# RWKV-7 attention and an exact-GELU block on one core: a new hand-written order of all steps, and a state turned with 40 weight columns

## The chip, the core and the metric

The kernel runs on one core of a Trainium2 chip. The metric is device time in microseconds. The kernel before was run three times: 655.43, 659.05 and 662.18 us, median 659.05.

## What is computed

The first half is a recurrence over 768 time steps for 4 batches and 8 heads of width 40. The second half takes its output as 3072 tokens of width 320 and puts them through two matrices with an exact GELU between.

```python
for t in range(S):                                   # S = 768, D = 40
    y[:, :, t] = einsum('bhd,bhde->bhe', rt, state)
    Sa = einsum('bhde,bhe->bhd', state, at)
    state = state * wt[:, :, None, :] - einsum('bhd,bhe->bhde', Sa, bt) \
            + einsum('bhd,bhe->bhde', vt, kt)
x = y.transpose(0, 2, 1, 3).reshape(B * S, H * D)    # (3072, 320)
h = x @ w_in                                         # w_in (320, 2048), float64
out = (0.5 * h * (1 + erf(h / sqrt(2)))) @ w_out     # w_out (2048, 320), float64
```

## The kernel before

Time is cut into 12 chunks of 64 steps, numbered 0 to 11. Within a chunk the recurrence becomes matrix products and the inverse of a triangular 64 by 64 matrix for each of the 32 pairs of batch and head. Each chunk then yields 256 tokens for the GELU block.

The kernel is written as small steps, each a Python generator whose pieces are issued one by one. `ORDER` (line 28) is a list of tokens written out by hand, such as `N9:2`: the next piece of step N of chunk 9, with duo 2 as its place. A duo is one of the four PSUM tiles of two banks (line 141); `conv` is one of three scratch tiles. The loop at line 1399 issues the tokens from left to right. Each of the engines PE, DVE, ACT, POOL and SP works its own instructions off strictly in the order in which the list brings them, and semaphores carry the dependencies between engines. The order of the list is thus the order of every queue, of SP's DMA issues too.

Steps of a chunk c that matter here, with their lines:

- `w`, `a`, `b`, `k`, `r`, `v`, `wq`, `vp`, `bp`, `kp` (246 to 311) load the inputs through SP's queue. `wi`, `wl`, `wo` load the two weight matrices (427 to 465), and `ci`, `co` turn their float64 words into float32 on DVE and ACT (492 to 502). They fill the first three chunks.
- `logs`, `sums`, `wt` (512 to 566) form the decays; `ta`, `tb`, `tk`, `tv`, `tr` (593 to 684) turn the inputs.
- `N` (714) multiplies on PE, masks on DVE (line 692), and stores the diagonal 32 by 32 blocks to DRAM with four issues. `nb` (796) loads them back with one matrix to a partition. `inv` (808) inverts them on POOL with 31 pairs of a product (line 819) and a sum (line 821) and stores the result (line 828; for chunk 3 and later POOL issues the store itself, before that SP). `ft` (837) loads the inverse, `corner` (924) turns a part on DVE (line 926) and multiplies on PE, and `joined` (938) completes the inverse `Tt`.
- `A`, `RV`, `av` (739 to 775) are products of inputs alone. `X` (955), `sa` (966), `QY`, `qk` (1047 to 1054) use the state; `state` (1107) writes the next one.
- `tn` (991) turns the state with PE and copies it to `turned` on ACT; `yy` (1020) multiplies with it, and `y` (1057) writes the tokens and moves some of their rows by DMA, partly through DRAM.
- `ph` (1205) is x @ w_in, from chunk 3 on with 7 half products for 8 (`pc`, `pd`, `pg` copy, add and apply the GELU); `po` (1286) is the product with w_out, from chunk 2 on likewise with sums on DVE.
- `warm` and `begin` (1382 to 1393) are products without use that keep PE going.

Every float32 product shows as two MATMUL records, a transpose as one. A group of 32 small products is thus 64 records.

Of the kernel before, what the change touches and what calls it, by code (L numbers as in the profile page):

```python
# [36 lines left out]
r2 tn1:2 r2 wi1 wi1 sc2 A1:0 A1 co0 y0:3 ci4:1 tables0 sums2 y0:1 y0 y0 RV1:0 wi1 wi1 RV1 ci4 inv1 tn1 tr2:1
tr2 ta2:2 co0 co1 tb2:0 ta2 av1:1:3 tb2 zeros8 yy1:2 inv3 wo2 yy1 ci4 ci6:0 yy1 ci6 k2 ci7:1 inv1 co1 inv2 wi1 v2
ci6 ci8:2 ph0:0 X1 N2:2 sk2 X1 ph0 ft1 N2 ci8 corner1:0 X1 ph0 ph0:1 corner1:2 ci8 ph0 ci7 wo4 ft1 zeros6 tk2:0 zeros7
corner1 co3:0 co3 co5:2 co5 co3 wo9 zeros5 ft1 ci7 tv2:2 co2:0 N2 tables0 co9:1 kp3 wo6 N2 a3 wq3 a3 wo15 tails1 kp3  # L40
tk2 A2:3 w3 nb2 wq3 nb2 b3 wo8 w3 A2 tv2 inv2 inv2 RV2:0 tables1 inv2 k3 inv2 RV2 co2 co2 co7:0 co9 ph0
ph0:2 joined1:0 joined1 ph0 co5 co7 co7 ph0 ph0:1 joined1 co4:0 sa1:0:2 co4 ta3 co6:2 ph0 sa1 sa1 co6 QY1:0:3 qk1 co6 co4 y1
state1 po0:2 co8:0 ph0 po0 co8 tn2:3 wo10 tn2 wt3:2 av2:0:1 co8 yy2:3 co9 y1 y1 wt3 co11:0 co11 yy2 yy2 wt3 logs3 y1
po0 po0 bp3 wt3 co15:1 vp3 co11 bp3 y1 vp3 vp3 tb3 wo14 tk3:2 co15 ta3 vp3 X2 ph1:3 co10:2 ph1 co14:0 X2 ph1
ph1:0 ph1 a4 N3:3 co10 tv3 a4 co14 wo12 co14 X2 wo13 co15 ph1 N3 co12:1 wq4 wq4 co12 co10 co12 sums3:1 ph1:0 r3
N3 ph1 N3 co13:2 inv2 r3 nb3 nb3 sums3 sk3 A3:3 inv4 co13 co13 wt4:1 ft2 ta4 inv3 po1:1 sc3 wt4 r3 ft2 ft2
po0 po0 corner2:2 ph1 po0 po0 A3 corner2:0 corner2 po1 joined2:0 vp4 ph1:3 wt4 r3 po0 po0 joined2 joined2 v3 tr3 sa2:0:2 bp4 ph1
w4 ph1 sa2 sa2 QY2:0:2 qk2 y2 state2 po1 bp4 RV3:3 RV3 po1 inv3 w4 vp4 vp4 po0 vp4 tv4 wt4 y2 kp4 kp4
tn3:2 av3:3:0 tn3 yy3:2 tb4 yy3 y2 y2 po1 yy3 X3 a5 ta4 tk4:1 wq5 po0 N4:2 inv3 po1 N4 y2 po1 wq5 N4
wt5:1 ph2:2 X3 ws0 N4 inv3 inv3 ph2 wt5 ph2 ph2:3 ph2 ph2 r4 r4 ph2:2 ww0:2 ww0 nb4 nb4 inv4 wt5 ft3 logs4  # L50
ft3 inv4 ft3 corner3:0 ph2 ws1 ww0 ph2 corner3:3 corner3 po1 ws3 joined3:3 r4 a5 r4 po1 ph2:2 po1 vp5 vp5 ws2 joined3 joined3
vp5 A4:1 ta5 X3 tr4 po1 sa3:3:0 sa3 sa3 ph2 vp5 A4 bp5 RV4:3 v4 kp5 ph2 kp5 QY3:0:1 qk3 inv4 po2:0 sums4:2 RV4
po2:3 y3 state3 sums4 k4 po2 tv5 b4 bp5 wt5 po2:1 tn4:1 po2 po2 y3 y3 av4:0:2 inv4 tn4 yy4:1 y3 ta5 yy4 yy4
tb5 wq6 po2:3 po2 N5:1 po1 wq6 a6 po2 po2 po2 X4 a6 N5 inv4 po2:3 y3 wt6:1 tk5:0 N5 N5 po2 X4 X4
po2 po2 po2:2 ft4 po2 nb5 tx3 tx3 sk4 tx3 A5:3 wt6 wt6 sc4 ph3:2 ft4 corner4:0 ft4 ph3:0 corner4:1 ta6 pc3 nb5 r5
pd3 tx3 ph3 inv5 corner4 tx3 joined4:0 pc3 r5 inv6 w5 A5 joined4 joined4 vp6 ph3:1 sa4:0:3 ww0 vp6 pg3 r5 bp6 ph3 pc3
sa4 r5 sa4 pd3 QY4:3:0 qk4 state4 tr5 ph3 pg3 w5 ph3 pd3 v6 pg3 y4 RV5:1 tn5:3 pg3 po3:0 po3:2 po3 vp6 inv5
RV5 logs5 v5 vp6 sums5:1 tn5 wt6 tv6 po3:1 po3 sums5 po2 yy5:3 yy5 ta6 inv5 kp6 yy5 av5:2:0 inv5 bp6 tb6 po3 po3:1
po3 po3 po3 po3 b5 inv5 kp6 po3:3 po3 y4 y4 N6:1 y4 tx4 a7 po3 wq7 wq7 tx4 N6 y4 tx4 a7 po3
inv5 X5 X5 N6 N6 k5 ft5 nb6 nb6 ph4:3 X5 ft5 ft5 sc5 pc4 ph4:0 ph4 pc4 wt7:1 wt7 ph4:2 ph4 sk5 tk6:0  # L60
r6 tx4 pd4 r6 inv6 corner5:0 ta7 corner5:0 r6 po3:1 inv6 inv6 wt7 po3 pg4 w6 corner5 po3 w6 warm4:0 tx4 pc4 joined5:1 joined5
# [14 lines left out]
ta10 ph7:1 r9 ph7 ft8 r9 pc7 ph7:0 ph7 ft8 r9 pc7 corner8:2 pd7 corner8 tx7 pd7 warm7:1 sk8 sc8 v9 vp10 joined8:2 joined8  # L76
r9 joined8 bp10 bp10 ph7 inv9 inv9 tx7 pd7 pg7 vp10 sa8:2:1 sa8 po6 ph7 w9 vp10 sa8 QY8:1:2 qk8 tr9 pg7 pg7 pg7
kp10 RV9:3 vp10 y8 state8 RV9 po7:0 po7:0 po7 tn9:2 y8 tv10 av9:3:1 wt10 po7:1 tn9 po7 po7 inv9 w9 ta10 y8 y8 yy9:0
yy9 wq11 po7:2 po7 yy9 po7 logs9 tx8 inv9 po7 po7 tx8 tx8 wq11 wt11:1 b9 tb10 po7:0 po7 kp10 sums9:2 wt11 po7 sums9
X9 tk10:0 inv9 N10:0 inv9 N10 X9 X9 k9 y8 ft9 sk9 ft9 ph8:2 N10 ph8:1 pc8 wt11 N10 ph8 corner9:0 corner9:0 ft9 pd8  # L80
r10 tx8 po7 corner9 po7:1 po7 joined9:0 nb10 nb10 sc9 inv10 joined9 joined9 r10 r10 tx8 pc8 ph8:3 sa9:0:1 sa9 inv11 r10 inv10 pg8
sa9 ph8 a11 a11 QY9:1:0 qk9 pc8 pd8 ph8 ta11 tr10 pd8 ph8 y9 w10 state9 pg8 pg8 po8:0 po8:3 pg8 po8 A10:0 k10
A10 wt11 tn10:1 RV10:2 vp11 po7 RV10 tn10 po8:1 po8 po8 po8:0 w10 yy10:2 kp11 bp11 v10 bp11 yy10 kp11 yy10 av10:3:1 po8 po8
vp11 inv10 po8 tb11 y9 y9 y9 logs10 tx9 po8 po8:2 vp11 vp11 ta11 tx9 inv10 po8 N11:0 X10 X10 po8 sums10:2 N11 y9
b10 X10 N11 ph9:0 N11 inv10 ph9:1 po8 pc9 nb11 tk11:1 r11 nb11 tx9 sums10 ph9 pc9 ph9:2 ph9 pd9 tv11 sc10 ft10 ft10
corner10:1 ft10 po8:1 pc9 sk10 w11 w11 corner10:3 po8 A11:1 corner10 r11 joined10:3 joined10 pd9 tx9 tx9 pg9 ph9 joined10 pd9 r11 pg9 pg9
po9:1 ph9 v11 sa10:2:3 sa10 r11 sa10 pg9 po8 tr11 po9:0 QY10:3:2 qk10 k11 logs11 A11 inv11 y10 po9 po9:0 inv11 po9 po9 po9:1
# [1349 lines left out]
```

## Time and profile before

| | |
|---|---|
| three runs, median | 659.05 us (655.43 to 662.18) |
| profiled execution, span | 653.2 us (its time outside the span is not given) |
| PE busy | 633.2 us |
| POOL busy | 387.0 us |
| DVE busy | 483.1 us |
| ACT busy | 274.7 us |
| granted TensorE clock, mean | 0.997 |
| DMA issues on SP's queue | 721 |
| ACT table loads in the program | 51 |
| products on PE in the program | 7112 |

The profile is one execution. In a timeline row stand the start in us, the duration in us, the engine, the line, the operation, the tiles written and read, the shape and the number of records; in brackets the idle time before it and what ended that. A line 154 is a helper's, so PE's steps are told apart by their tiles: `aT,nT` is N, `st,aT` is X, `ident,st` is tn, `conv,N` and `conv,spare` are corner, `Tt,Js` is joined. A row of the waits has the total in us, the number of times and the longest. In a row of the chain that ended last stand the start, the duration and what was at work.

### The profile page before, as it was taken

How to read it: one execution, taken by the hardware profiler on the slowest of the kernel's cores; microseconds unless marked ns; L12 is line 12 of the kernel's file. 1: busy time of each engine (PE TensorE's matmuls, PEld its weight loads, DVE VectorE, ACT ScalarE, POOL GpSimd, SP SyncE). 2: the span in 40 equal slices, each digit the busy share in tenths (PEclk: the TensorE clock that was granted, in tenths of full speed). 3: DMA queues.
4: the chain of work that ended last, by engine and by line, in shares of the span. 5: the costliest groups of instructions: out<-in, count | busy, mean ns of one | idle time of the engine just before them, and what ended most of it. 6: DMA issues, size and time to landing. Idle time of an engine off the chain costs nothing.

```text
span 653.2 us, 31493 instructions
## 1 busy us (share of the span) xinstructions
PE 633.2 (97%) x14128; PEld 573.0 (88%) x14128; DVE 483.1 (74%) x643; ACT 274.7 (42%) x327; POOL 387.0 (59%) x797
## 2 busy tenths in 40 slices
PE   9998999989999999999999999999999999999997
PEld 5887788766888989999989989999999998998987
DVE  1697999997687997875976988886895874834442
ACT  4365574553334333515534345444433445135130
POOL 5258624865857865846857856868834877811000
PEclk9999999999999999999999999999999999999999
DMA  9999989568576776877776767696577865330100
GB/s 128 167 173 182 192 182 177 134 148 148 106 141 118 137 129 123 150 141 114 141 145 116 134 115 146 126 162 129 111 132 146 134 125 96 60 71 5 31 12 21
DMA packets 299111, 80.76 MB, mean 124 GB/s; under 512 B 287688, under 2 KB 292560, under 8 KB 298976
## 3 DMA queue, kind: packets, MB, share of 16 engines
q1 hardware_dynamic: 297872, 76.23, 63.5%
q0 software_dynamic: 864, 2.36, 2.1%
q8 instruction: 110, 1.80, 1.2%
q14 instruction: 25, 0.20, 0.1%
q10 hardware_dynamic: 240, 0.16, 0.1%
HBM read 65.40 MB, written 11.01 MB: 117 GB/s over the span
## 4 chain that ended last, share of the span: by engine, by line
PE 65%; POOL 10%; DMA 8%; SPq 6%; DVE 5%; issue 4%; ACT 2%; DVEq 0%; POOLq 0%; ACTq 0%
PE duo L154 25%; PE duo L1310 15%; PE duo L1216 10%; PE duo L1191 6%; SPq L222 6%; POOL tmp L819 5%; POOL W L821 5%; PE duo L1294 4%; PE duo L1223 3%; PE duo L572 2%; DMA Tt<-inv 2%; DMA inv<-W 2%; DMA Nb<-N 1%; DMA rows<-in_k_dram 1%; DMA inv<-rT 1%
## 5 line engine op out<-in xcount | busy, mean ns | idle before, releaser
L819 POOL TENSOR_TENSOR tmp<-W,Nb 128x56 f32<-128x56 f32 (+22 forms) x155 | 77.5, 500 | 60.5 <-DMA Nb<-N 48.7
L1310 PE MATMUL duo<-w_out_sb,gt 128*128 128x160 f32 x640 | 93.2, 302 | 1.9 <-ACT gt L1268 1.2
L819 POOL TENSOR_TENSOR tmp<-rT,Nb 128x56 f32<-128x56 f32 (+22 forms) x155 | 71.3, 460 | 35.7 <-DMA Nb<-N 23.9
L1310 PEld LDWEIGHTS duo<-w_out_sb,gt 128*128 128x128 f32 x640 | 87.7, 190 | 5.0 <-ACT gt L1268 1.4
L821 POOL TENSOR_TENSOR W<-W,tmp 128x56 f32<-128x56 f32 (+22 forms) x155 | 77.2, 498 | 12.1
L821 POOL TENSOR_TENSOR rT<-rT,tmp 128x56 f32<-128x56 f32 (+22 forms) x155 | 74.1, 478 | 12.1
L1216 PE MATMUL duo<-xt,w_in_sb 64*128 64x128 f32 x864 | 61.5, 275 | 0.0
L1254 ACT COPY gt<-duo 128x1024 f32<-128x1024 f32 x27 | 27.3, 1011 | 72.9 <-PE duo L1216 46.3
L1260 DVE TENSOR_TENSOR gt<-gt,duo 128x1024 f32<-128x1024 f32 x27 | 32.8, 1213 | 32.9 <-ACT gt L1254 17.3
L1223 PE MATMUL duo<-xt,w_in_sb 64*128 64x128 f32 x576 | 56.2, 272 | 0.0
L1191 PE MATMUL duo<-xt,w_in_sb 64*128 64x256 f32 x480 | 55.6, 382 | 0.6 <-ACT SM L962 0.4
L1216 PEld LDWEIGHTS duo<-xt,w_in_sb 64*128 64x128 f32 x864 | 54.1, 188 | 1.7 <-DVE spare L692 0.5
L1191 PEld LDWEIGHTS duo<-xt,w_in_sb 64*128 64x128 f32 x480 | 45.3, 187 | 7.6 <-ACT SM L962 0.8
L1310 PE MATMUL duo<-extra,conv 128*128 128x160 f32 x320 | 46.8, 302 | 0.5 <-issue 0.5
L1310 PEld LDWEIGHTS duo<-extra,conv 128*128 128x128 f32 x320 | 43.9, 190 | 1.6 <-issue 0.9
L1223 PEld LDWEIGHTS duo<-xt,w_in_sb 64*128 64x128 f32 x576 | 44.1, 188 | 0.0
L621 POOL TENSOR_TENSOR rows<-rows,w_tile 128x640 f32<-128x640 f32 x9 | 15.6, 1737 | 43.6 <-ACT w_tile L537 29.4
L1266 ACT ACTIVATE gt<-gt 128x1024 f32<-128x1024 f32 x27 | 28.2, 1056 | 29.3 <-DVE gt L1260 29.0
L1294 PE MATMUL duo<-w_out_sb,gt 128*128 128x320 f32 x128 | 37.0, 440 | 0.5 <-ACT w_tile L537 0.5
L1294 PEld LDWEIGHTS duo<-w_out_sb,gt 128*128 128x128 f32 x128 | 23.5, 190 | 10.2 <-ACT w_tile L537 0.6
L1314 DVE TENSOR_TENSOR os<-os,duo 128x160 f32<-128x160 f32 x40 | 12.7, 317 | 24.9 <-PE duo L1310 22.2
L962 ACT COPY SM<-duo 128x832 f32<-128x832 f32 (+1 forms) x22 | 17.4, 827 | 26.8 <-PE duo L154 26.8
(257 smaller groups left out, 1420.1 us busy)
## 6 DMA issues: line engine op xcount, KB each, us to landing
Nb<-N SPq DMA_DIRECT2D x18, 256.0 KB
VR<-in_v_dram SPq DMA_DIRECT2D x24, 160.0 KB
out_dram<-os SPq DMA_DIRECT2D x45, 80.0 KB
rows<-in_b_dram SPq DMA_DIRECT2D x22, 160.0 KB
rows<-in_k_dram SPq DMA_DIRECT2D x22, 160.0 KB
w_out_sb<-in_moe_w_out_dram SPq DMA_DIRECT2D x5, 640.0 KB
w_tile<-in_w_dram SPq DMA_DIRECT2D x36, 80.0 KB
Tt<-inv SPq DMA_DIRECT2D x44, 64.0 KB
```

Of the source, the lines that this page charges most:

```text
L154: nc.tensor.matmul(o, lhsT, rhs, start=first, stop=True, skip_group_check=True)
L222: queue[0].dma_start(out=out, in_=in_)
L819: eng.tensor_tensor(t, W[:, :nr, j:j + 1].to_broadcast([P, nr, rest]), Nb[:, j:j + 1, j + 1:].to_broadcast([P, nr, rest]), ALU.mult)
L821: eng.tensor_tensor(W[:, :nr, j + 1:], W[:, :nr, j + 1:], t, ALU.add)
L1191: nc.tensor.matmul(pt[:, x, s], w_in_sb[half(x), kt, p * P:(p + 1) * P], xt[half(x), kt], start=kt == 0, stop=kt == NK - 1)
L1216: nc.tensor.matmul(out_of(pt)[:, x, j], left(kt, j)[half(x)], right[half(x), kt], start=first and j == 0 and kt == 0, stop=True, skip_grou ...
L1223: nc.tensor.matmul(out_of(pt)[:, x, j], w_in_sb[half(x), NP, at:at + P], xt[half(x), NP, cols], start=False, stop=True, skip_group_check=True)
L1254: nc.scalar.copy(block_of(f, g), out_of(of(c)["u"]))
L1260: nc.vector.tensor_tensor(block_of(f, g), block_of(f, g), out_of(of(c)[v_]), ALU.add)
L1266: nc.scalar.activation(block_of(f, g), block_of(f, g), ACT.Gelu)
L1294: nc.tensor.matmul(pt[:, g], gt[:, f, g * P:(g + 1) * P], w_out_sb[:, f], start=f == 0, stop=f == NF - 1)
L1310: nc.tensor.matmul(pt[:, n, :DM // 2], l_[:, f], r_[:, f], start=f == 0, stop=f == NF // 2 - 1)
```

## The change

Two edits.

First, `tn` for chunks 3 and later. Its 32 products turn 40 by 40 pieces of the state: the state's columns are the weights, an identity of 40 columns streams through. Before, 64 weight columns were loaded for each piece, so that 64 rows came out, of which later steps read 40. Now 40 columns are loaded, and the copy covers partitions 0 to 103.

```diff
-                        mm(pt[half(g), x, e * NP + i], st[half(x, D), e, i, g, :HP], ident[half(x, D), half(x, D)])
+                        mm(pt[half(g, D), x, e * NP + i], st[half(x, D), e, i, g, :D], ident[half(x, D), half(x, D)])
...
-        nc.scalar.copy(turned[:, :TW].rearrange("p (n x d) -> p x n d", x=2, d=D), pt)
+        nc.scalar.copy(turned[:HP + D, :TW].rearrange("p (n x d) -> p x n d", x=2, d=D), pt[:HP + D])
```

Second, `ORDER` is replaced as a whole. The same 1554 tokens stand in it, in another order and with other places. All instructions are the same but tn's; the program has 53 ACT table loads in place of 51 and 108 separate semaphore waits on PE in place of 96. A few lines around the inversion of chunk 9, before and after:

```diff
-y7 RV8:0 inv8 inv8 bp9 y7 tn8:3 pg6 po5 po6 wt9 tn8 RV8 tv9 po6:0 av8:3:0 tb9 y7 y7 po6 inv8 yy8:2 kp9 ta9
-kp9 yy8 wq10 po6 po6:1 wq10 po6 yy8 N9:2 po6 po6 po6 X8 X8 N9 po6:1 tk9:0 y7 N9 N9 po6 logs8 wt10:1 inv8
-b8 tx7 tx7 po6 po6 po6:3 sums8:1 po6 inv10 wt10 nb9 tx7 nb9 wt10 X8 A9:0 A9 ft8 a10 corner8:0 a10 sums8 ph7:3 pc7
...
+po6 y7 yy8 tb9 k8 logs8 po6:0 y7 kp9 yy8 po6 inv8 po6 po6 X8 N9:3 po6 inv8 X8 N9 sums8:0 inv8
+po6:2 wt10:0 inv8 wt10 sums8 y7 tk9:1 po6 N9 tx7 N9 ph7:3 tx7 pc7 po6 sc8 r9 ft8 sk8 nb9 tx7 ph7:0
+corner8:1 ph7 nb9 pd7 pc7 a10 inv9 po6 ft8 ph7:2 wt10 ph7 w9 tx7 X8 vp10 ft8 po6:0 r9 po6 pc7 corner8:1
```

What the new order moves, as far as the prediction speaks of it:

- In PE's queue, between N(c) and the product of corner(c). Chunk 2: out go a piece of ph0, the first quarter of po1 and four quarters of po0; in come X1 and a warm product. Chunk 4: out go two quarters of po1 and a half product of po2; in comes X3. Chunk 5: out go X4 and three pieces of ph4; in comes a half product of po3. Chunk 7: out goes X6. Chunk 9: out go X8 and two pieces of ph8 (one of 48 records, one of 32). Chunk 10: in come two half products of po7 and one small step.
- In SP's queue: from the first store of N2 to the first load of nb2 there are 10 issues (18 before); the store of inverse 2 stands ahead of N3's stores (behind before); the first pair of ft8 stands ahead of nb9 (behind before), and the first pair of ft3 between the two loads of nb4 (behind both before). The first issues are wi1, w0, w1, a0, b1, b0 (before: w0, w1, b0, a0, r0, b1). v11 moves from po8's and po9's steps to the last steps.

More of the change, by code (lines that the diff above doesn't have):

```diff
@@ L37 @@
[L37 to L61, printed above, removed]
@@ L77 @@
[L77 to L86, printed above, removed]
@@ new lines @@
+yy3 av3:3:2 yy3 tb4 tables1 po1 y2 po1 ta4 N4:1 inv3 wq5 X3 w4 po1 wq5 N4 wt5:0 w4 X3 po1 tk4:1
+a5 y2 X3 inv3 N4 N4 ph2:1 ws3 inv3 inv3 wt5 vp5 ph2 nb4 ph2 ww0:2 ft3 nb4 corner3:1 ph2:3 a5 ph2
+inv4 corner3:2 r4 ta5 corner3 ph2 ft3 po1 ft3 vp5 ph2:1 ph2 joined3:2 wt5 ph2 bp5 inv4 A4:0 joined3 r4 ph2:3 joined3
+r4 sa3:1:2 r4 A4 v4 ph2 tr4 kp5 RV4:0 po1 sa3 sa3 vp5 RV4 po1 inv4 QY3:1:2 logs4 ph2 qk3 sums4:0 po2:1
+state3 vp5 po2:3 sums4 tn4:0 po2 b4 y3 av4:1:2 bp5 kp5 wt5 tv5 ta5 po2:0 tn4 po2 yy4:0 y3 y3 po2 yy4
@@ new lines @@
+A9 w9 logs9 QY8:1:0 kp10 RV9:2 RV9 vp10 inv9 qk8 pg7 state8 bp10 y8 warm7:3 po7:1 b9 po7:2 inv9 av9:3:1 tn9:0 kp10
+bp10 wt10 inv9 y8 po7 tn9 yy9:0 ta10 v10 po7:0 po7 yy9 y8 vp10 po7 po7:2 yy9 po7 po6 y8 tb10 inv9
+X9 k9 po7 N10:0 po7 X9 po7 sums9:2 tv10 tk10:1 tx8 y8 po7:3 sums9 sk9 N10 X9 ft9 tx8 wq11 ft9 corner9:0
+po7 ph8:2 ft9 tx8 po7 corner9:1 pc8 wq11 corner9 N10 ph8:0 a11 ph8 pc8 pd8 tx8 wt11:1 tx8 joined9:3 po7 joined9 a11
+po7:1 wt11 sc9 ph8:0 joined9 po7 inv10 N10 sa9:3:1 ph8 r10 sa9 sa9 nb10 QY9:3:1 nb10 wt11 pc8 qk9 r10 r10 pd8
@@ new lines @@
+ph8 state9 pd8 ph8 po7 r10 pg8 tr10 pg8 y9 pg8 A10:0 po8:0 ta11 po8:3 tn10:1 pg8 RV10:2 po8 wt11 tn10 inv11
+RV10 po8:1 inv10 po8 kp11 po8 vp11 inv10 po8:1 w10 yy10:2 A10 ta11 yy10 po8 vp11 y9 inv10 po8 po8 po8 av10:3:0
+y9 bp11 po8:1 vp11 bp11 y9 vp11 kp11 tx9 k10 po8 tb11 y9 yy10 tk11:0 w10 po8 inv10 N11:2 X10 X10 X10
+tx9 N11 b10 logs10 ph9:1 tx9 pc9 ph9:3 tx9 pd9 sums10:2 po8 N11 po8:0 N11 ph9 inv10 r11 nb11 ph9:3 pc9 sums10
+ph9 pc9 ft10 tv11 nb11 ft10 r11 corner10:1 corner10:2 corner10 po8 pd9 r11 tx9 pg9 ft10 A11:0 ph9 joined10:2 sc10 A11 sk10
@@ L94 @@
+po10:0 po10 po10 y11 po10 po10 po10:3 tx11 po10 ph11:2 y11 y11 tx11 po10 ph11:1 po10 tx11 y11 pc11 tx11 pd11 ph11
+tx11 ph11:0 pc11 pg11 ph11 po10:3 pc11 v11 po11:1 pd11 pg11 po10 ph11 ph11 pd11 pg11 pg11 po11:1 po11 po10 po11:0 po11
+po11 po11:3 po11 po11 po11 po11 po11:0 po11 po11 po11 po11 po11:2 po11 po11
 """
```

77 lines of the change are left out of this document (50 added, 27 removed).

## The prediction

> **What bounds the kernel now.** I read the page's busy times first, then who waited for whom, then the chain that ended last and the timelines of PE, POOL, SP and DVE around the steps that have moved.
>
> ```profile
> span 653.2 us, 31493 instructions
> PE 633.2 (97%) x14128; PEld 573.0 (88%) x14128; DVE 483.1 (74%) x643; ACT 274.7 (42%) x327; POOL 387.0 (59%) x797
> ```
>
> PE is busy for 97% of the span, and the two programs hold the same 7112 matrix products. A new order can therefore win only what PE now loses in waits, while it can lose any amount. What it loses now, 15 rows in all:
>
> ```profile
> PE duo L154 <- issue: 5.4, 6, 3.0
> ...
> PE duo L154 <- DVE w_in_sb L1388: 1.5, 1, 1.5
> ...
> PE duo L154 <- DMA Tt<-inv: 0.2, 1, 0.2
> ```
>
> The 15 rows add up to 15.8 us. 1.5 of them are the first memset, which no order avoids; 14.3 us are left to win.
>
> The one long dependency that PE's filler work must cover in every chunk is the inversion: N(c) on PE, its mask on DVE, four stores to DRAM and two loads on SP's queue, 62 small operations on POOL, a store, the loads of ft(c), a turn on DVE, and then corner(c) on PE. Chunk 10 shows it; the first row is N10 from PE's timeline, the others are from the chain that ended last, where the one but last is the inverse's way to DRAM and the last begins with corner10:
>
> ```profile
> 480.82 1.16 PE L154 MATMUL duo<-aT,nT 40*64 40x64 f32 x64 [0.17 <-DVE os L1314]
> ```
> ```profile
> 533.83 5.38 DMA inv<-W
> ...
> 544.44 2.53 PE duo L154 x164
> ```
>
> That is 63.6 us from N10 to corner10. Other engines wait for the same chain in most chunks (total, times, longest):
>
> ```profile
> POOL tmp L819 <- DMA Nb<-N: 72.6, 9, 19.5
> DVE conv L926 <- DMA Tt<-inv: 18.8, 8, 5.8
> ```
>
> POOL stood waiting for its matrix nine times and DVE for the inverse eight times, so in most chunks the chain runs without slack and PE only just has enough other work.
>
> **Part 1: PE's order between N(c) and corner(c).** The times of four windows now, N first and corner second (chunks 2, 4, 7, 9):
>
> ```profile
> 83.56 1.11 PE L154 MATMUL duo<-aT,nT 40*64 40x64 f32 x64
> ...
> 157.26 0.75 PE L154 MATMUL duo<-conv,N 32*32 32x32 f32 x64
> ```
> ```profile
> 183.37 1.11 PE L154 MATMUL duo<-aT,nT 40*64 40x64 f32 x64
> ...
> 246.74 0.75 PE L154 MATMUL duo<-conv,N 32*32 32x32 f32 x64
> ```
> ```profile
> 328.37 1.16 PE L154 MATMUL duo<-aT,nT 40*64 40x64 f32 x64
> ...
> 390.92 0.75 PE L154 MATMUL duo<-conv,spare 32*32 32x32 f32 x64 [0.34 <-DVE conv L926]
> ```
> ```profile
> 425.71 1.16 PE L154 MATMUL duo<-aT,nT 40*64 40x64 f32 x64
> ...
> 488.37 0.75 PE L154 MATMUL duo<-conv,spare 32*32 32x32 f32 x64
> ```
>
> They last 73.7, 63.4, 62.5 and 62.7 us. Chunk 7's corner already makes PE wait 0.34 us for DVE: 62.5 is a tight chain. Now the prices of the steps that the new order takes out of these windows or puts in:
>
> ```profile
> 202.75 2.42 PE L1294 MATMUL duo<-w_out_sb,gt 128*128 128x320 f32 x8
> 205.10 0.75 PE L154 MATMUL duo<-Tt,Js 32*32 32x32 f32 x64
> ...
> 210.66 2.43 PE L1191 MATMUL duo<-xt,w_in_sb 64*128 64x256 f32 x20
> ```
> ```profile
> 484.47 0.61 PE L1216 MATMUL duo<-xt,w_in_sb 64*128 64x128 f32 x8
> ...
> 485.14 0.61 PE L1216 MATMUL duo<-xt,w_in_sb 64*128 64x128 f32 x8
> ...
> 486.48 1.95 PE L1216 MATMUL duo<-rT,rows 64*128 64x128 f32 x32
> ...
> 489.05 2.44 PE L1310 MATMUL duo<-extra,gt 128*128 128x160 f32 x16
> ```
> ```profile
> 285.51 1.61 PE L154 MATMUL duo<-st,aT 40*64 40x104 f32 x64
> ```
>
> In that order: a quarter of an early po costs 2.35 us from start to start (those of po0 and po1 lie a little lower), a piece of an early ph 2.2 to 2.4, ph's 48-record piece 2.68 (four times 484.47 to 485.14), its 32-record piece 1.8 to 1.9, a half-product of a later po 2.4, and X, whose last record runs a little into the next group, 1.5.
>
> Chunk 2 loses ph0's second piece, the first quarter of po1 and four quarters of po0 (13.3 us) and gains X1 and a warm-up product (2.5): 73.7 becomes 62.9. Chunk 4 loses two quarters of po1 and one half-product of po2 (6.7) and gains X3 (1.5): 63.4 becomes 58.2. Chunk 7 loses X6: 62.5 becomes 61.0. Chunk 9 loses X8 and two pieces of ph8 (6.0): 62.7 becomes 56.7. Chunk 5 loses 5.5 by the same count, but chunk 4's stall at its corner falls inside that window and covers it. The other windows lose 2.2 us at most or grow, and I cost them at nothing.
>
> How long is the chain in the new order? POOL's operations stay as they are. Chunk 2 has waits on SP's queue that the new order takes out (N's first store and the first load back; POOL's last operation and the store of its result):
>
> ```profile
> 88.38 0.83 SPq L222 DMA_DIRECT2D N<-N  x2
> ...
> 101.61 2.33 SPq L222 DMA_DIRECT2D Nb<-N  x2
> ```
> ```profile
> 142.28 0.23 POOL L821 TENSOR_TENSOR W<-W,tmp 128x16 f32<-128x16 f32 x1
> ```
> ```profile
> 146.52 1.29 SPq L828 DMA_DIRECT2D inv<-W  x2
> ```
>
> The 18 issues from 88.38 to 101.61 become 10, about 5 us less; and the store, which stood 4 us behind N3's stores, comes ahead of them. So 73.7 becomes about 64.7, and PE waits 64.7 - 62.9 = 1.8. For the others I keep the chain that was measured: chunk 4 waits 63.4 - 58.2 = 5.2, chunk 7 1.5, chunk 9 6.0. Sum 14.5.
>
> Two bounds. The shortest chain in the trace is that of chunk 11, late, when few transfers run:
>
> ```profile
> 526.84 1.16 PE L154 MATMUL duo<-aT,nT 40*64 40x64 f32 x64
> ```
> ```profile
> 584.19 0.71 DVE L926 STREAM_TRANSPOSE conv<-Tt 128x512 f32<-128x512 f32 x1
> ```
>
> It could have started corner11 at 584.9, after 58.1 us. With 58.1 everywhere, chunk 9 alone waits, 1.4 us. Upwards, SP's order makes chunk 9 worse:
>
> ```profile
> 435.98 1.58 SPq L222 DMA_DIRECT2D Nb<-N  x2
> 438.84 0.84 SPq L222 DMA_DIRECT2D Tt<-inv  x2
> ```
>
> The load of Nb for chunk 9 was issued 2.9 us before ft8, which waits for inverse 8. In the new order ft8's first pair stands ahead of it, so POOL would begin inverse 9 up to 4 us later. In chunk 4 one of the two Nb loads likewise stands behind ft3.
>
> **Part 2: waits that go.** Where PE comes later than before, some of the 14.3 us are over by then. I take a third, 4.5 us; the ends are 0 and 14.3.
>
> **Part 3: 40 weight columns.** tn(c) for c of 3 to 11, nine times 32 products. The rows, each group running to the start of the next:
>
> ```profile
> 265.12 1.16 PE L154 MATMUL duo<-rT,late 40*64 40x64 f32 x64
> 266.10 1.09 PE L154 MATMUL duo<-ident,st 40*64 40x40 f32 x64
> 267.12 4.61 PE L1310 MATMUL duo<-w_out_sb,gt 128*128 128x160 f32 x32
> ...
> 297.97 0.75 PE L154 MATMUL duo<-conv,spare 32*32 32x32 f32 x64
> 298.65 1.62 PE L1310 MATMUL duo<-extra,gt 128*128 128x160 f32 x10
> ```
>
> tn streams only 40 columns, yet takes 1.02 us, no less than the group before it that streams 64 (0.98): with 64 weight columns, the loads set its pace. 64 records with 32 weight columns take 0.68. On the line between, 40 columns cost 0.76: 0.26 saved, nine times 2.3 us. Ends: 0 (the pace is something else) and 9 x 0.34 = 3.1. The Trainium skill, page "TensorE: Matmul & The Clock Gate", speaks against the gain in its section "Wait — 56ns, not 53.3ns?": start to start never falls below about 25 ns however few columns stream. By that rule 64 records would need 1.6 us, the saving would be 0 and the sum 2.3 us higher; the trace disagrees, since 0.68 us for 64 records is 10.6 ns each. The copy of the turned state goes to 104 partitions in place of 128 with as many elements in each, so I cost it at nothing.
>
> **Part 4: the start, and ACT.**
>
> ```profile
> 5.56 1.28 ACT L514 ACT_TABLE_LOAD   x1 [5.56 <-DMA w_tile<-in_w_dram]
> ```
>
> ACT's first operation waits for w0, now SP's first transfer. In the new order a piece of w_in goes ahead of it, and b0 is the fifth pair of loads in place of the third. One issue is about 0.75 us (435.98 above: 1.58 for two), and the piece's bytes share the way; against that, PE's warm-up covers some of it. I take +0.7, one issue (ends 0 and twice that). ACT gets two more table loads, 1.28 us each; at 42% busy it hides them (ends 0 and 2.6). PE waits on a semaphore by itself 12 times more (108 for 96); the 5.4 us that PE stood without a reason shown, over 96, bound that at 0.06 us each, 0.7, and I take 0. The load of v11, which chunk 11 does not need, moves on SP from among po8's and po9's steps to the last ones: 1.6 us for two issues that the last products cover. The remaining moves on DVE and ACT have no row that prices them; I cost them at nothing, with DVE's slack (74% busy) as cover; if that is gone, PE's waits for DVE, now among the 14.3 us, grow.
>
> **Sum.** 14.5 - 4.5 - 2.3 + 0.7 = +8.4 us on the span of 653.2. The three runs before have a median of 659.05, 5.9 above that span, so I add the difference to the median: 667.5 us.
>
> **Rivals.**
> Longer chain: ft8 ahead of Nb9 costs its 4 us, and chunk 2's front gains only half of its 9 us, so 4.5 more. 667.5 + 8.5 = 676. For it: SP issues back to back around N9. Against it: inverse 8 may end earlier relative to N9 than now.
> No change: chains of 60.5 us, midway between 58.1 and the tight 62.5 to 63.6. Chunk 4 waits 2.3, chunk 9 3.8, the others nothing: 6.1 - 4.5 - 2.3 + 0.7 = 0, 659.
> Faster (the other side): the chain reaches chunk 11's 58.1 us in all chunks because SP serves N, Nb and ft sooner. It decides once the chain is under 60.5. 1.4 - 4.5 - 2.3 + 0.7 = -4.7, 654; with twice as much of the old waits gone, 650. Against it: nowhere but in chunk 11, with the transfers nearly over, is it that short.
>
> **How the numbers follow.** Forecast (667.5, itself 662 to 672) 0.36, longer chain 0.18, no change 0.28, faster 0.18. About 1%, 6.6 us, is what a measurement here can tell from none: 652.5 and 665.6. Slower by more: 0.30 of the forecast's 0.36, and the longer chain's 0.18, 0.48 together. Faster by more: somewhat under the faster rival's share, 0.14. Within: 0.38. The range runs from 652, where the chain is short, to 677, where SP's order lengthens it; one end each keeps a tenth outside.
>
> **What would show it.** Right: in the new trace PE's or PEld's waits for DVE L926 or Tt<-inv come to 8 to 15 us, with single waits of some us ahead of corner4 and corner9, and tn's groups last near 0.76 us. Wrong: corner4 and corner9 come 58 us after N4 and N9 with no wait (then the chain has slack that I denied it), or the new waits lie in the first 150 us, or tn still lasts 1.02.

## The result, and the profile after

| | before | after |
|---|---|---|
| four runs each, median | 660.62 us (655.43 to 666.76) | 682.50 us (676.81 to 685.14) |
| profiled execution: time, span | -, 653.2 us | 685.14, 683.4 us |
| PE busy | 633.2 us | 645.5 us |
| granted TensorE clock, mean | 0.997 | 0.983 |

The ratio is 1.036, 95% interval 1.032 to 1.041: slower, by 21 to 27 us where 8.4 were forecast. The runs of a kernel vary by 1%: the profiled execution of after is the slowest of its four and that of before a quick one, so the traces are 30.2 us apart where the medians are 21.9 apart, and the trace of the second kernel in experiment 5, a disturbed execution, is not used.

First the page of after, its first lines:

```profile
span 683.4 us, 31517 instructions
...
PE 645.5 (94%) x14128; PEld 579.5 (85%) x14128; DVE 480.9 (70%) x643; ACT 276.7 (40%) x329; POOL 384.9 (56%) x797
```

The span grew by 30.2 us. 12.3 of that are PE's busy time, though PE does the same products and tn got shorter; the other 17.9 are PE's waits. The waits of after, longest first (18 rows in all, their sum 33.7 us; before 15 rows and 15.8):

```profile
PE duo L160 <- DVE conv L932: 8.5, 4, 4.2
PE duo L160 <- issue: 7.9, 4, 5.2
PE duo L160 <- DMA Tt<-inv: 3.4, 4, 1.3
PE duo L578 <- DVE extra L619: 2.2, 1, 2.2
PE duo L1316 <- ACT os L1341: 2.1, 1, 2.1
```

The first and the third row, 11.9 us, are the end of the inversion's chain (the turn ahead of corner, the inverse ahead of joined). The second is PE standing with nothing shown that it waits for. Where they lie, from PE's timeline:

```profile
70.22 3.04 PE L160 MATMUL duo<-VR,extra 64*64 64x104 f32 x60 [5.23 <-issue]
...
211.34 0.87 PE L160 MATMUL duo<-conv,spare 32*32 32x32 f32 x49 [4.16 <-DVE conv L932]
...
257.85 0.75 PE L160 MATMUL duo<-conv,N 32*32 32x32 f32 x64 [1.12 <-DVE conv L932]
264.02 1.24 PE L160 MATMUL duo<-Tt,Js 32*32 32x32 f32 x64 [1.07 <-DMA Tt<-inv]
...
316.04 0.90 PE L160 MATMUL duo<-Tt,Js 32*32 32x32 f32 x60 [1.33 <-DMA Tt<-inv]
...
509.89 0.75 PE L160 MATMUL duo<-conv,spare 32*32 32x32 f32 x64
...
572.17 0.74 PE L160 MATMUL duo<-conv,N 32*32 32x32 f32 x64 [2.76 <-DVE conv L932]
```

These are qk0, corner3, corner4, joined4, joined5, corner9 and corner10. The long waits stand at corner3 and corner10, whose windows the prediction had costed at nothing; corner4 waits 1.1 us and corner9 not at all. At corner10 the chain itself is longer: from N10 (501.78) to the issue of its Nb load (519.86) it takes 18.1 us, where before took 11.0 (480.82 to 491.78). The mask on DVE came 5.5 us after N10 (2.5 in before), and the four stores, in a row in before, are split: the second pair stands at 515.34, behind three pairs of other transfers.

And the part of the loss that no list of waits shows. The windows view of after for the five stretches in which the granted clock (the third number from the right) was halved; behind the length of the stretch stands PE's busy time:

```profile
18.20:21.60 3.40, 3.40 (x67) 1.83 (x65) 0.60 (x1) 0.99 (x1) 0.00 (x0) 0.50 1.15 152
55.70:59.10 3.40, 3.40 (x38) 3.07 (x34) 1.64 (x3) 2.78 (x4) 2.93 (x7) 0.50 1.22 132
69.40:76.20 6.80, 5.98 (x99) 4.23 (x101) 3.25 (x8) 0.70 (x2) 5.55 (x17) 0.50 0.52 87
209.30:216.10 6.80, 4.76 (x82) 4.03 (x84) 2.59 (x4) 1.30 (x2) 2.64 (x10) 0.50 1.07 143
574.50:577.90 3.40, 3.40 (x38) 3.40 (x36) 0.97 (x1) 1.19 (x2) 2.71 (x9) 0.50 0.18 31
```

PE was busy for 20.9 us in them, at half speed: 10.5 us lost by that count. The records that begin in them took 20.6 us, and at their mean durations in before they would take 10.0. Before had one such stretch, 1.7 us, behind its longest wait:

```profile
62.29 0.48 PE L154 MATMUL duo<-VR,extra 64*64 64x104 f32 x9 [3.04 <-issue]
```
```profile
63.30:66.70 3.40, 3.40 (x35) 2.02 (x29) 3.40 (x9) 0.23 (x1) 2.85 (x8) 0.50 1.24 168
```

The longer ones of after stand at the long waits: 69.4 inside that of 5.23, 209.3 inside that of 4.16, 574.5 behind that of 2.76. So the 30.2 us are: waits +17.9, halved clock +8.8, tn -1.9, and +5.4 of other PE busy time that I could not assign.

### The profile page after: what moved, and what is told of

It is laid out like the page before. It is cut to its first block, busy times and chain, and to the rows that moved or that the text cites. A ratio compares the mean times of both kernels' runs of the same rounds, so it can differ in the third digit from the quotient of the medians.

```text
span 683.4 us, 31517 instructions
## 1 busy us (share of the span) xinstructions
PE 645.5 (94%) x14128; PEld 579.5 (85%) x14128; DVE 480.9 (70%) x643; ACT 276.7 (40%) x329; POOL 384.9 (56%) x797
## 4 chain that ended last, share of the span: by engine, by line
PE 45%; POOL 20%; DMA 11%; SPq 11%; issue 7%; DVE 5%; ACT 1%; DVEq 0%; POOLq 0%; ACTq 0%
PE duo L160 19%; SPq L228 11%; PE duo L1316 10%; POOL tmp L825 10%; PE duo L1222 7%; POOL rT L827 5%; POOL W L827 5%; PE duo L1197 5%; DMA Nb<-N 4%; PE duo L1229 2%; PE duo L1300 1%; PE duo L578 1%; DMA Tt<-inv 1%; DMA inv<-W 1%; DMA inv<-rT 1%
## 5 line engine op out<-in xcount | busy, mean ns | idle before, releaser
L825 POOL TENSOR_TENSOR tmp<-W,Nb 128x56 f32<-128x56 f32 (+22 forms) x155 | 71.3, 460 | 70.0 <-DMA Nb<-N 58.3
L825 POOL TENSOR_TENSOR tmp<-rT,Nb 128x56 f32<-128x56 f32 (+22 forms) x155 | 76.2, 491 | 47.6 <-DMA Nb<-N 35.8
L827 POOL TENSOR_TENSOR W<-W,tmp 128x56 f32<-128x56 f32 (+22 forms) x155 | 81.4, 525 | 12.1
L827 POOL TENSOR_TENSOR rT<-rT,tmp 128x56 f32<-128x56 f32 (+22 forms) x155 | 72.7, 469 | 12.1
L1222 PE MATMUL duo<-xt,w_in_sb 64*128 64x128 f32 x864 | 62.5, 276 | 0.0
L1229 PE MATMUL duo<-xt,w_in_sb 64*128 64x128 f32 x576 | 58.0, 276 | 1.2 <-DVE xt L1188 1.2
L1197 PE MATMUL duo<-xt,w_in_sb 64*128 64x256 f32 x480 | 57.1, 391 | 0.0
L1222 PEld LDWEIGHTS duo<-xt,w_in_sb 64*128 64x128 f32 x864 | 54.7, 188 | 2.2 <-issue 1.3
L1197 PEld LDWEIGHTS duo<-xt,w_in_sb 64*128 64x128 f32 x480 | 47.5, 192 | 6.8 <-ACT gt L1201 0.5
L1229 PEld LDWEIGHTS duo<-xt,w_in_sb 64*128 64x128 f32 x576 | 45.4, 190 | 1.7 <-DVE xt L1188 1.6
```

The lines of the kernel that those rows point to most:

```text
L825: eng.tensor_tensor(t, W[:, :nr, j:j + 1].to_broadcast([P, nr, rest]), Nb[:, j:j + 1, j + 1:].to_broadcast([P, nr, rest]), ALU.mult)
L827: eng.tensor_tensor(W[:, :nr, j + 1:], W[:, :nr, j + 1:], t, ALU.add)
L1197: nc.tensor.matmul(pt[:, x, s], w_in_sb[half(x), kt, p * P:(p + 1) * P], xt[half(x), kt], start=kt == 0, stop=kt == NK - 1)
L1222: nc.tensor.matmul(out_of(pt)[:, x, j], left(kt, j)[half(x)], right[half(x), kt], start=first and j == 0 and kt == 0, stop=True, skip_grou ...
L1229: nc.tensor.matmul(out_of(pt)[:, x, j], w_in_sb[half(x), NP, at:at + P], xt[half(x), NP, cols], start=False, stop=True, skip_group_check=True)
```

## The experiments

All ratios are to before on the same chip, with 95% intervals; 1% is 6.6 us. "Lag" is how far PE is behind its own work at a place: the start of a step there less the sum of all earlier steps' durations, each at its mean duration, waits left out, in before's trace (tn's shorter groups in that of experiment 1).

**1. The edit of tn alone**, run twice.

```diff
-  mm(pt[half(g), x, e * NP + i], st[half(x, D), e, i, g, :HP], ident[half(x, D), half(x, D)])
+  mm(pt[half(g, D), x, e * NP + i], st[half(x, D), e, i, g, :D], ident[half(x, D), half(x, D)])
```

> The order before, with the edit of tn alone (40 weight columns from chunk 3 on). Record's part 3 (nine groups shorter by 0.26 us each): 2.0 to 2.3 us faster than before, tn groups of 0.7 to 0.8 us in place of 0.91 to 1.02. Rival (a product does not get shorter with fewer weight columns): no change.

> The order before with the edit of tn alone again, as the base for the three kernels beside it on the same chip. First run: 0.9978 of before, interval 0.9938 to 1.0019. Part 3 on record: 2.0 to 2.3 us faster, 0.9965. If it is no change: 1.000.

Measured 0.9978 (0.9938 to 1.0019) and 1.0008 (0.9979 to 1.0037): no change that can be told. The groups did get shorter, as here in the second run, where tn runs to the start of the next group:

```profile
264.70 0.81 PE L154 MATMUL duo<-ident,st 40*40 40x40 f32 x64
265.45 1.76 PE L1310 MATMUL duo<-w_out_sb,gt 128*128 128x160 f32 x11
```

0.75 us where it was 1.02. The nine groups sum to 6.1 us in the first run, 8.7 in before. In both traces PE's wait inside X6 was 2.0 to 2.2 us (0.89 before) and was followed by a halved stretch, 1.7 us, that before does not have:

```profile
330.84 0.67 PE L154 MATMUL duo<-st,aT 40*64 40x104 f32 x20 [1.96 <-issue]
```

So in these traces 2.6 us were saved and about as much was given back at one place. The saving is 0.4% of the time, and the intervals are too wide to show or to exclude it.

**2. The head and the rest, apart.** The first product of N2 is the cut. First the order of before up to the cut, then what is left in the order of after (the diff is to before, at the cut):

```diff
-ci8:2 ph0:0 X1 N2:2 sk2 X1 ph0 ft1 N2
+ci8:2 ph0:2 X1 tails1 ci7 zeros6 ph0 ph0 ci7 N2:1 sk2 co3:1 N2
...
```

> The order before up to the first product of N2, then all that is left in the order after. In the trace of after, PE stands 11.6 us further behind its own work at N2 than in the trace of before, and about 19 us more are lost after it. If the start's loss adds up (start theory): 11 to 12 us faster than after, about 671. If the later loss is waits for the chain of a chunk that would only begin earlier by as much, or that swallow the start's loss (corner theory, as on record: the loss lies at the corners and nowhere else): within 3 us of after, 680 to 684.

The other way round (the diff is to after):

```diff
-ph0 ph0 ci7 ci8:2 N2:1 co1:0 inv1 sk2 co3:1 N2
+ph0 ph0 ci7 ci8:2 warm0:1 co1:0 co1 inv3 inv1 co1 inv2 X1 N2:0 sk2 X1 ft1 N2
...
```

> The order after up to the first product of N2, then all that is left in the order before; tn as after. Start theory, loss adds up: before plus 11.6 minus 2.2, about 670. If the waits behind it swallow the start's loss: about 658 to 661.

Measured 1.0404 (1.0319 to 1.049) and 1.0166 (1.0091 to 1.024). Read together these looked as if the rest costs everything and the head 12 us more. But both kernels have a flaw: I gave the steps PSUM places by the rest's list, so that the head had the places of the other order. In the first of them PE's lag grew by 6 us more between N1 and qk0 than in before. Experiment 3 measures that.

**3. Places alone.** The order before with tn's 40 columns; ahead of N2 the steps take the PSUM places that after gives them.

```diff
-gaps0 sums0:0 sums0:1 v0
+gaps0 sums0:1 sums0:2 v0
...
-sc0 sums1 ta0 tb0:0 warm1:3 r0 warm6:1 sc1
+sc0 sums1 ta0 tb0:1 warm1:2 r0 warm6:2 sc1
```

> The order before with tn's 40 columns, in which alone the PSUM places of 40 odd tokens ahead of N2 are those that after gives to the same steps. The first run with before's head had these places and lost 6 us more between N1 and QY0 than before, with 3.5 us of PE's waits for ACT's copy of w_in_sb. If the places cost what that run showed: 4 to 7 us slower than with 40 columns alone, about 1.006 of before. Rival (the waits behind it swallow it): no change.

Measured 1.0169 (1.012 to 1.0218): some 10 us from place numbers alone. In its trace (of an execution of 660.5 us) PE's lag at N2 is 14.9 us, 8.0 with the own places. In its first 90 us PE waits 7.2 us for ACT and DVE, against nothing but the first memset's 1.5 with the own places: a place that another order would have free is still being read here. Places belong to an order; this says nothing against those of after in their own order, but it spoils the second experiment.

**4. The head with its own places.** Once more after's head and before's rest, and that with the first loads in the sequence of before.

```diff
-ci6 ph0:0 k2 tables0
+ci6 ph0:2 k2 tables0
...
-co1 inv2 X1 N2:0 sk2 X1 ft1 N2
+co1 inv2 X1 N2:2 sk2 X1 ft1 N2
```

> The order and the PSUM places of after up to the first product of N2, then all that is left in the order and the places of before; tn with 40 columns. The earlier kernel with this head had other places in it, and alien places alone cost 1.7% in another kernel. In the traces of after, PE was 11 us further behind its work at N2 than in before, 6 to 7 at N4. Start theory: 6 to 11 us slower than before with 40 columns alone (1.000), 1.009 to 1.017. Rival (nearly all of that is swallowed or was due to places): under 1.005.

```diff
-consts0 wi1 w0 logs0 w1 a0 b1 b0 sums0:1 wi0 sums0:2
+consts0 w0 w1 logs0 b0 a0 r0 b1 sums0:1 a1 sums0:2
```

> The kernel beside it (head of after with its own places, rest of before), in which the first loads stand in SP's queue in the sequence of before (w0, w1, b0, a0, r0, b1, a1, wi1, wi0). If the late b0 sets the head's loss: sc0 starts 2.5 to 3 us earlier and the kernel is 3 to 5 us faster than the one beside it. Rival: within 2 us of it.

Measured 1.0099 (1.0064 to 1.0134) and 1.0145 (1.0091 to 1.0199). The head costs 6 us, at the low end, and the late b0 is not what makes it so: with the loads as before sc0 begins at 14.27 (16.34 without that) and nothing is won. The same edit had been tried on the flawed kernel:

> The kernel with the head of after and the rest of before (1.017 of before), in which the first loads stand in SP's queue in the sequence of before: w0, w1, b0, a0, r0, b1, a1, wi1. Start theory: sc0 starts at 13.3 us in place of 16.1, N1 3 us earlier, and 3 to 5 us faster than that kernel, about 1.011 of before. Rival (the head's loss lies in PE's order and places between N1 and N2): within 2 us of that kernel.

Measured 1.0205 (1.0148 to 1.0262), no gain either. What the head of after does show, in this kernel as in after, is the longest wait "for nothing" at the same instruction, the fifth record of qk0:

```profile
68.49 2.80 PE L154 MATMUL duo<-VR,extra 64*64 64x104 f32 x60 [4.40 <-issue]
```

**5. SP's sequence.** First for all chunks, then from chunk 4 on alone. Only issues of nb, ft, N's stores (and inverse 2's) move, among themselves. For chunks 4 and 11, the second kernel:

```diff
-ph2 nb4 ph2 ww0:2 ft3 nb4 corner3:1
+ph2 nb4 ph2 ww0:2 nb4 ft3 corner3:1
...
-r11 nb11 ph9:3 pc9 sums10 ph9 pc9 ft10 tv11 nb11 ft10
+r11 nb11 ph9:3 pc9 sums10 ph9 pc9 nb11 tv11 ft10 ft10
```

> The order after, in which only the issues of nb, ft, the stores of N and the store of inverse 2 stand in SP's queue in the sequence of before among themselves; the other engines' queues are those of after. SP theory (in chunks 4, 6, 9, 10, 11 loads of the inverse stand ahead of nb or of N's stores and make the chain from N to corner longer): from N's end to the inversion's start 13 to 16 us in place of 18 to 22, and 6 to 10 us faster than after, about 674. Corner theory (steps of PE are gone from the windows, the chain's length is as before): within 2 us of after.

> The order after, in which the issues of nb, ft and N's stores stand in SP's queue in the sequence of before among themselves, from nb4 and ft3 on alone (the run before this one had that for all chunks: from N4 on it lost 12 us less than after, and between N2 and N4 it lost 12 us more). SP theory: 11 to 13 us faster than after, about 1.018 of before, with 58 us from N4 to corner4 in place of 64.4 and 62 to 63 from N11 to corner11 in place of 66.2. Corner theory: as after, 1.036 of before.

Measured 1.0356 (1.0281 to 1.043) and 1.0244 (1.0211 to 1.0277). The first looks like nothing and is two effects that cancel: its lag grows by 10 us between N2 and N4, where after's is flat (20.0 and 18.7), and from N4 to corner11 by 17 where after's grows by 29. Most of the 10 us is a wait of 8.2 us at corner2, and the clock was halved for 10.2 us from 152.6 on. In chunks 2 and 3 the new sequence is the better one; from chunk 4 on it costs. The second kernel keeps the better half and is 1.2% faster than after. Chunk 4 shows the mechanism. SP in after, then POOL's first operation on the loaded matrix:

```profile
202.63 0.45 SPq L228 DMA_DIRECT2D Nb<-N  x1
207.88 0.84 SPq L228 DMA_DIRECT2D Tt<-inv  x2
208.77 0.49 SPq L228 DMA_DIRECT2D Nb<-N  x1
```
```profile
212.75 0.23 POOL L825 TENSOR_TENSOR tmp<-W,Nb 128x31 f32<-128x31 f32 x1 [6.88 <-DMA Nb<-N]
```

and the same two in the kernel that has before's sequence in all chunks:

```profile
206.44 1.09 SPq L222 DMA_DIRECT2D Nb<-N  x2
207.62 1.07 SPq L222 DMA_DIRECT2D Tt<-inv  x2
```
```profile
211.30 0.23 POOL L819 TENSOR_TENSOR tmp<-W,Nb 128x31 f32<-128x31 f32 x1 [18.68 <-DMA Nb<-N]
```

In after the second half of Nb stands behind ft3, which waits some 5 us for inverse 3, and POOL for it. From N4 (193.41 and 198.88) to POOL's first product it takes 19.3 us in after, 12.4 here. N4 to corner4 falls from 64.4 to 57.7 in this kernel. (In the two kernels built on the mended one, experiments 7 and 11, it is still 62: there ft4 stands on SP behind the stores of N5, which come later.)

**6. The counterpart:** before's order with tn's 40 columns, and after's sequence of the same issues from chunk 4 on.

```diff
-ww0:2 ww0 nb4 nb4 inv4 wt5 ft3 logs4
+ww0:2 ww0 nb4 ft3 nb4 inv4 wt5 logs4
```

> The counterpart: the order before with tn's 40 columns, in which the same issues stand in SP's queue in the sequence of after from nb4 and ft3 on. PE's queue, and with it every window from N to corner, is that of before. SP theory: 6 to 12 us slower than before with 40 columns (654), 660 to 666, since the chain gets some 6 us longer in chunks 4, 6 and 11, where PE has 61.8, 64.2 and 61.2 us of work to cover it. Corner theory: within 2 us of 654, since no step of PE has left a window.

Measured 1.0076 (1.0045 to 1.0107): 4 to 6 us slower than tn alone, with no step of PE moved. Both directions agree on 4 to 8 us for this sequence.

**7. Before's head, with its own places, on the kernel with the mended sequence.**

```diff
-ci6 ph0:2 k2 tables0 ph0 ph0 ci7 ci8:2 N2:1 co1:0 inv1 sk2 co3:1 N2
+wi1 v2 ci6 ci8:2 ph0:0 X1 tails1 ci7 zeros6 ph0 ph0 ci7 N2:2 sk2 co3:1 N2
...
```

> The order and the PSUM places of before up to the first product of N2, then all that is left as in the kernel with the SP sequence restored from chunk 4 on (the earlier run with this head had the places of after in it, and lost 6 us between N1 and QY0 that before doesn't). Start theory, the loss at the start adds up: 10 to 12 us faster than that kernel, about 1.002 of before. If the waits behind swallow it: as that kernel, about 1.018.

Measured 1.0257 (1.0219 to 1.0294), as without it. The head's 6 us in front of before's rest do not show in front of after's. Its trace has a lag of 7.4 us at N2 and 12.5 at N4. The kernel of experiment 11, which has the other head and the same order up to N4, has 17.4 and 16.6, so more than half of what is won at N2 is gone at N4. The two losses do not add up; why the rest of that difference does not show in the runs stays open.

**8. The corners alone.** Before's order with tn's 40 columns; two pieces of ph3 go behind corner4's product and two of ph8 behind corner9's.

```diff
-sc4 ph3:2 ft4 corner4:0 ft4 ph3:0 corner4:1 ta6
+sc4 ft4 corner4:0 ft4 corner4:1 ph3:2 ph3:0 ta6
...
-N10 ph8:1 pc8 wt11 N10 ph8 corner9:0 corner9:0 ft9
+N10 pc8 wt11 N10 corner9:0 corner9:0 ph8:1 ph8 ft9
```

> The order before with tn's 40 columns, in which alone PE's queue changes at two places: two pieces of ph3 (1.9 and 2.7 us) stand behind corner4's product and two of ph8 (2.7 and 1.8 us) behind corner9's, where they stood ahead of it. That is the prediction's part 1 at its two largest corners, without anything else of the change. Corner theory: stalls of about 6 us ahead of corner4 and 4.7 us ahead of corner9 (1.5 and 0.2 in before), 8 to 9 us slower than before with 40 columns alone, about 1.011 of before. Rival (the steps that come later give PE work where it would have waited at joined or sa): within 3 us of before with 40 columns.

Measured 1.0171 (1.0118 to 1.0223). Part 1 of the prediction in its pure form: 4.6 and 4.5 us of work leave the windows, and PE waits as long. The two waits in the rows here are 5.5 and 3.7 us longer than with tn alone (0.57 and 0.31), 9.2 together:

```profile
247.36 0.87 PE L154 MATMUL duo<-conv,N 32*32 32x32 f32 x48 [6.03 <-DVE conv L926]
...
498.66 0.75 PE L154 MATMUL duo<-conv,spare 32*32 32x32 f32 x64 [4.01 <-DVE conv L926]
```

But the kernel loses 11 us, not 9.1, and its profiled execution, 670.4, lost 16. The windows view has the rest: the stretch of the wait, and the one behind it, in which the clock was halved for 10.2 us:

```profile
240.00:243.40 3.40, 1.33 (x66) 1.02 (x64) 3.00 (x5) 0.00 (x0) 2.93 (x5) 1.00 0.66 124
243.40:253.60 10.20, 6.24 (x112) 6.18 (x114) 4.79 (x5) 1.29 (x2) 1.74 (x7) 0.50 0.64 110
```

**9. The same waits, filled with useless work.** Experiment 8 with nine products that nothing reads.

```diff
-corner4:0 ft4 corner4:1 ph3:2 ph3:0
+corner4:0 ft4 warm20:1 warm21:0 warm22:2 warm23:1 warm24:0 corner4:1 ph3:2 ph3:0
...
-corner9:0 corner9:0 ph8:1 ph8
+corner9:0 warm25:0 warm26:3 warm27:1 warm28:0 corner9:0 ph8:1 ph8
```

> The kernel with the two shorter windows and nothing else moved, to which products without use (some 0.9 us each) are added in PE's queue, five ahead of corner4's product and four ahead of corner9's, where PE stood for 5.8 and 4.7 us. The waits themselves stay. In that kernel's trace the granted clock was halved for three stretches of 3.41 us behind corner4 and one behind corner9. Clock theory (a stretch of 3.41 us in which PE is busy less than about half is followed by one at half the clock): no halved stretch behind the two corners, and 3 to 6 us faster than that kernel (1.017 of before), 1.008 to 1.012. Rival (the halved clock costs nothing, since PE waits for the chain anyway): no change, or slower by what the added products stick out.

Measured 1.0102 (1.0065 to 1.014): 0.7% back, by adding work. The intervals overlap; the clock is plainer. Its mean over the six timed runs was 0.985 in experiment 8 (0.981 to 0.992) and is 0.996 here (0.994 to 1.000), as high as in before. The same two stretches in the trace:

```profile
240.00:243.40 3.40, 2.80 (x68) 1.89 (x69) 3.17 (x8) 0.00 (x0) 1.48 (x6) 1.00 0.73 130
243.40:253.60 10.20, 10.20 (x214) 8.21 (x214) 5.61 (x7) 1.43 (x3) 3.15 (x11) 1.00 0.84 146
```

Full clock, and nearly twice the records done in the second, some six of them useless. (The corner came 1.2 us earlier there, which helps.) At corner9 the first useless product had itself to wait 2.0 us for its PSUM place and cost one halved stretch there.

**10. The same in after.**

```diff
-ph2 inv4 corner3:2 r4
+ph2 inv4 warm29:2 warm30:1 warm31:2 warm32:1 corner3:2 r4
...
-corner10:1 corner10:2
+corner10:1 warm34:2 warm35:2 corner10:2
```

One more each stands ahead of joined3 and joined10.

> The order after, to which the same products without use are added: four ahead of corner3's product, one ahead of joined3, two ahead of corner10's product and one ahead of joined10, where PE stood for 4.3, 2.0, 2.8 and 1.7 us in the trace of after. No wait is taken away. Clock theory: the halved stretches at 209 to 216 us and at 575 us go, three of 3.41 us, some 5 us faster than after (1.036 of before), about 1.028. Rival (the waits alone are the loss): as after.

Measured 1.0296 (1.0255 to 1.0337), after 1.036 (1.032 to 1.041) in another set of runs; the intervals overlap a little, and the mean clock over the runs rose only from 0.987 to 0.990. Behind corner3 the clock stays up (in after 0.50 and 4.76 us of PE's time for 82 records):

```profile
209.30:216.20 6.90, 6.90 (x168) 5.35 (x168) 5.07 (x5) 3.62 (x4) 6.00 (x12) 1.00 0.57 103
```

The edit takes no wait of the chain away, and some 0.66%, 4.4 us, came back: close to the three stretches of 1.7 us that had been named, but by itself weaker evidence than experiment 9. (In this execution PE then waits 3.1 us at corner4, and two halved stretches stand there instead.)

**11. Corners later.** On the kernel with the mended sequence, corner9's product goes behind two pieces of ph8 and corner5's behind one of ph4.

```diff
-corner9:1 pc8 wq11 corner9 N10 ph8:0 a11 ph8 pc8
+pc8 wq11 N10 ph8:0 a11 ph8 corner9:1 corner9 pc8
```

> The kernel with the SP sequence restored from chunk 4 on, in which the products of corner9 and of corner5 stand later in PE's queue: behind two pieces of ph8 (2.7 and 1.8 us) and behind one piece of ph4 (1.8 us), so that the windows from N to corner have that much more work, and nothing else is moved. Corner theory: the stall of 4.2 us ahead of corner9 goes and 1.8 of the 4.6 ahead of corner5, 5 to 6 us faster than the kernel without this. Rival (the steps that wait behind the corner are late by as much, so that the wait comes back at joined or sa): no change.

Measured 1.0284 (1.0238 to 1.0331), the base 1.0244: no gain, the rival's outcome. In its trace PE does not wait for the turn at corner5 and corner9 (it does at corner3, 2.6 us); it waits 3.1 and 0.7 us for the inverse at joined5 and joined9. The window of corner9 has 4.5 us more work and takes 63.3 us. Here later corners only moved the loss.

## Why the prediction was wrong

The direction was right; the size was not. On the traces the span grew by 30.2 us where 8.4 were forecast. Of the difference, Part 2 makes 12.2 us, the clock, which had no term, 8.8, and 5.4 could not be assigned; Part 1 came out 4.3 smaller than forecast. The terms against the profiled executions (the rows of Part 4 and of SP's sequence are effects on the runs' time and lie within the others):

| step | forecast | measured |
|---|---|---|
| Part 1, stalls at the corners | +14.5 | +10.2 in after (11.9 of waits for the turn or the inverse, 1.7 before); 5.5 and 3.7 at two corners when tested alone, for 4.6 and 4.5 of work |
| Part 2, old waits that go | -4.5 | +7.7 (all other waits: 14.1 before, 21.8 after) |
| Part 3, tn | -2.3 | -1.9 in its groups |
| Part 4, the start | +0.7 | +6 alone (0.9%) |
| SP's sequence | 0, as a rival 4 | 4 to 8 |
| clock | none | +8.8 |

**Part 1 held as a rule and failed as a map.** What leaves a tight window comes back as a wait, about us for us: experiment 8 shows it. Two forecast lengths were close: N4 to corner4 64.4 us (63.4 forecast), N7 to corner7 63.1 (62.5). Chunk 4's is partly luck. POOL began 19.3 us after N4, 14.7 in before, and from POOL's last operation to the corner it took 8.5 us, 11.5 in before, so two changes nearly cancel. N9 to corner9 took 60.6 us without a wait, where 62.7 with a wait of 6.0 had been forecast. The waits were to lie ahead of corner4 (5.2) and corner9 (6.0) and lay ahead of corner3 (4.16) and corner10 (2.76). A window is over when chain and PE's time are both over, and PE loses time inside it elsewhere: in chunk 4's window lie corner3's wait of 4.16 and the halved stretch behind it, so that only 1.1 was left to wait for at corner4. I had said this of chunk 5 and not of chunk 4. Chunk 3 I had costed at nothing because it loses "2.2 us at most"; with no slack in a chain 2.2 us cost 2.2 us; that is about half of its 4.16, and the other half was not traced. Chunk 10's chain grew by 6.8 us (70.4 from 63.6), all of it between N10 and POOL's start, which no term priced. By the prediction's own test (8 to 15 us of such waits: 11.9) the mechanism passes, by its places it does not. Of the 17.9 us by which PE's waits grew, 3.7 lie in the first 150 us.

**SP's sequence was seen and not priced.** "In chunk 4 one of the two Nb loads likewise stands behind ft3" stands there without a number, and the 4 us for chunk 9 only in a rival. In chunk 4 POOL starts 6.9 us later than with before's sequence in the same order; the whole sequence is worth 4 to 8 us (experiments 5 and 6). For chunk 2, the gain on SP was read rightly: 58.9 us from N2 to corner2, even less than the 64.7 forecast.

**Part 2 has the wrong sign.** A third of the old waits, 4.5 us, was to go because PE comes later. That much did go: rows of before worth 5.1 us have no counterpart in after. But the new order brings 12.8 us of its own, and for these there was no term: 2.2 us for sc0 (DVE L619 behind b0), 2.1 for ACT at L1341, 2.2 us more for "issue", and ten smaller rows.

**Part 4 weighed one load.** The late b0 is real (sc0 begins at 16.11, it did at 13.26), and PE waits 2.2 us for it, but the head's 6 us are not undone by loading it earlier. I cannot say which step of the head makes them; the longer wait inside qk0 is the largest single row.

**The clock is the step that is missing altogether,** and the one that the readers should keep. The profile of before had it: 0.997 on average and one halved stretch, right behind its wait of 3.04 us. The Trainium skill, page "TensorE: Matmul & The Clock Gate", section "HAM oscillation — how this bites in real kernels", has the rule 'The abstract rule is "no PE-idle gaps >~3.4µs."' and its section "What's actually happening" gives the window as 3413 ns. The traces agree with the window (every halved stretch within a span is 3.41 us or a multiple) and are stricter than the rule: the wait of 2.76 us at corner10 sufficed. The prediction used that page of the Trainium skill for tn and not for the waits that it forecast. By experiment 8, where half clock cost 3.1 and 1.5 us behind waits of 6.0 and 4.0 us, each wait of 4 to 6 us in Part 1 should have carried an estimated 1.5 to 3 us more.

**Part 3 was right** in size and in its reason: fewer weight columns, shorter groups. The floor of about 25 ns from start to start, which the prediction cites from the Trainium skill, does not bind in this layout: 64 records took 0.62 to 0.75 us in the first run of experiment 1. The saving does not show in the run time; it is within the noise, and in both traces a wait behind it grew.

No version tried here beats the kernel before by more than the runs vary.

## What to carry to other kernels

When PE is the bound, price a wait on it twice: its length, and the half-speed stretch that follows if PE was busy for less than about half of some 3.41 us. Useless products in the wait can bring the second part back (0.7% in experiment 9), and they are a cheap test of whether the clock is part of a loss; in both tests here a wait of 2 to 3 us appeared or grew elsewhere. When a long chain of small operations runs beside PE without slack, look at the queue of every engine on it, SP's above all: one issue that waits, put ahead of one that doesn't, lengthens the chain by its wait, and a hybrid of two orders must keep each order's own buffer places or it measures those.

## What the runs showed of the hardware

**The clock follows the busy share on a fixed grid.** Over the seventeen traces I cut PE's time into stretches of 3.413 us on the grid that the halved ones show, and left out those that were themselves halved. Of 29 stretches in which PE was busy for less than 40%, all 29 were followed by a halved one; at 40 to 50% 10 of 14, at 50 to 60% 8 of 29, at 60 to 70% one of 46, and above 70% none of more than 3000. The one above 60% is corner10's in after: 69% busy, behind one of 50%, so the share of a single stretch does not settle it. A wait of about 2 us can thus halve the clock or not: 1.96 us inside X6 did in experiment 1, 2.11 us at L1341 in after did not. The clock goes along with the differences between runs of one kernel: tn's kernel took 650.7 us at a mean clock of 0.997 and 660.6 at 0.992, and that of experiment 8 661.8 us at 0.992 and 670.4 at 0.982.

**PE stops at fixed instructions.** The wait inside qk0 comes behind the 4th of its 64 records in all eight traces with after's head (1.70 to 5.23 us) and behind the 55th in all nine with before's (0.45 to 3.04). It names no releaser. In after it lasts from 65.0 to 70.2 us; in the trace's list of transfers one of 16 KB on the queue "instruction" begins at 67.47 and takes 1.25 us, and nothing else on that queue begins between 57.4 and 71.9. The one inside X6 (2.0 us in experiment 1) has such a transfer too, from 328.06 to 329.52, and ends at 330.84. The Trainium skill, page "Runtime: NRT & Kernel Launch", section "Terms", says that an engine's instruction memory is refilled in 16 KiB blocks; the size fits, and no run here tested whether PE waited for it. Such transfers are frequent (111 in after's 683 us, one in 6 us on average), and the one beside qk0 ended 1.5 us before PE went on, so the cause stays open.
